# Two sums of a Strassen block written to PSUM, and the mixture's products issued in the order of the code

## The chip, the cores and the metric

The kernel runs on one core of a Trainium2 chip. Its engines work side by side: TensorE (PE in the profile, its weight loads PEld), VectorE (DVE), ScalarE (ACT), GpSimd (POOL) and SyncE (SP), which issues the DMA transfers. The metric is the device time of one execution in microseconds, lower is better; for the kernel before, the median of three runs is given.

## The reference

Banded attention with a few global columns gives x, 3072 tokens by 512; a mixture of eight experts follows, whose mixing weights are a matrix of token by expert, normalized alternately along its rows and columns, eight times.

```python
x = attention(q, k, v)                  # 4*768 tokens, 8 heads * 64
logits = x @ w_gate                     # 3072 x 8
P = np.exp(logits - logits.max())
for _ in range(8):
    P /= P.sum(1, keepdims=True) + 1e-09
    P /= P.sum(0, keepdims=True) + 1e-09
    P *= N / E
for e in range(8):
    h = np.maximum(x @ w1[e], 0.0)      # 3072 x 1024
    out += P[:, e:e + 1] * (h @ w2[e])  # 3072 x 512
```

## The kernel before

**Tiling.** The tokens are cut into eight units of 384 (`NU`, three tiles of 128 each), and two units make a block b. Every operand of a product is split into a high and a low half, so that each product is three matmuls: high by low, low by high, high by high (`products`, L617 to L619; `layer2`, L685 to L687). The attention comes first, with the first experts' work on units 0 to 6 woven between its steps. From about 380 us on only the mixture is left, in this order of the code in `pipeline`:

- **The last filler**, `filler(NU - 1, ...)`: for unit 7 and the first four column groups (f = 0 to 3) of expert 0, 48 matmuls into `h_ps` (384 columns each), four `relu_split`, then for each of three token tiles twelve matmuls into `y_ps` (512 columns, L698 to L700), each tile copied out by ScalarE (L810).
- **The gate** of unit 7: eight matmuls into `g_ps` (L710), a copy by ScalarE to `g_sb` (L713), three transposes (`gt_ps`, L717).
- **The loop over 120 steps.** A step takes one group g of weights (two column groups of an expert) and one block b. `layer1_strassen` computes the hidden values of the block's two units and the group's two column groups by Strassen's scheme: seven products m1 to m7, six matmuls of 384 columns each, 42 in all, into four PSUM banks in the order m3 to c, m2 to d, m1 to a, m6 to b, m5 to c, m4 to d, m7 to a. Between them ScalarE copies bank c (L658) and VectorE adds and subtracts (L660 to L671), and the four hidden blocks are split by `relu_split`: ScalarE's Relu gives the high half `hh` (L625), VectorE the low half `hl` (L626). `second` then does the second layer of the step before: six token tiles of six matmuls with 512 columns (36 in all) into `y_ps`, each added to its accumulator by VectorE (L933 for expert 0, L937 with the mixing weight for the others).
- **The normalization** `sinkhorn` is a generator of which `second` calls the next piece after the first, fourth and sixth tile. Each of its eight iterations is a chain on VectorE (L742 to L745, then L750 to L754) with one matmul between, `c_ps` (L748), which sums the columns over the partitions. When it is done, the accumulators of expert 0 are multiplied by its mixing weight on ScalarE, two blocks of six (L936).

**Pools.** The four banks a to d come from `mps` with four buffers, so the next step's banks are the same four; `yps` has three, `sps` (for g_sb's transposes and c_ps) one. `hpool` holds eight hh and eight hl.

**Weights.** Each group's weights are loaded by SyncE's queue into a single staging buffer, summed by GpSimd, cast to the high half by ScalarE (L537) and subtracted to the low half by GpSimd (L538), a step or two ahead.

**What sets the order.** Every instruction is recorded in the order of the code, and a scheduler then places the instructions of all engines by times that it estimates itself, unless one is held in the order of the code. `InOrder` does that: its `matmul` and `transpose` issue on TensorE and hold what they issue in program order. The attention uses it (`attention.pe`), and `moe.pe` is set to it while the attention runs; at L875 `moe.pe` becomes plain `nc.tensor`, so that the scheduler is free with the products of the mixture from there on. On each engine instructions start in the order in which they finally stand.

## Time and profile before

| what | value |
|---|---|
| median of 3 runs | 2286.73 us (2285.66 to 2288.38) |
| the profiled execution | 2288.16 us |
| its span in the trace | 2286.3 us |
| granted TensorE clock, mean | 0.989 of full speed |
| TensorE busy | 2236.0 us, 98% of the span |
| VectorE busy | 1560.3 us, 68% |
| GpSimd busy | 823.5 us, 36% |
| ScalarE busy | 696.2 us, 30% |
| chain that ended last, TensorE's share | 90% |
| first product of the loop's first step | starts at 398.98 us |

The span is the time from the first to the last instruction of one profiled execution. Busy shares are means over stages that differ; what an edit is worth is read in its own stage, from what TensorE waits for there. A row of the timeline gives start, duration, engine, line, operation and, in brackets, the idle time before it and who ended it. Durations of matmuls are modelled, and consecutive ones overlap; the distance from start to start is what a product costs. Matmuls carry the lines of the helper that issues them: L617 to L619 in `products`, L685 to L687 in `layer2`, L698 to L700 in `layer2_wide`.

### The profile page before, as it was taken

To read this page: it belongs to the slowest core of one execution; us is meant where nothing else is said; L and a number is where in the kernel's file an instruction comes from. 1 tells how busy PE (TensorE), PEld (TensorE's weight loads), DVE (VectorE), ACT (ScalarE), POOL (GpSimd) and SP (SyncE) were. 2 spreads that over 40 slices of the span, in tenths; PEclk is the share of its full clock that TensorE was granted. 3 is DMA by queue.
4 is the path that set the end of the run, shared out by engine and by line. 5 is a ranking of instruction groups with operands and counts; after the bars stand their busy time and mean duration, and the time that the engine had idled before them with its cause. 6 is when DMAs were issued, how large, how long until landed. Compare 5 with 4: busy or idle time off the path is not lost.

```text
span 2286.3 us, 31486 instructions
## 1 busy us (share of the span) xinstructions
PE 2236.0 (98%) x12147; PEld 1991.2 (87%) x12147; DVE 1560.3 (68%) x2746; ACT 696.2 (30%) x1528; POOL 823.5 (36%) x655
## 2 busy tenths in 40 slices
PE   7989989999999999999999999999999999999998
PEld 5777878898998998998998998998998999989987
DVE  6566666886766666766666667666766666666665
ACT  5655654332222222222222224222222222222221
POOL 4165283432333333333333234333333233333320
PEclk8999999999999999999999999999999999999999
DMA  6455433110111011111001361101110101110101
GB/s 163 116 163 145 125 85 95 32 43 28 37 38 38 28 30 36 38 37 37 28 29 38 129 239 39 36 28 38 37 38 28 37 28 38 37 37 28 35 22 57
DMA packets 177615, 133.75 MB, mean 59 GB/s; under 512 B 117040, under 2 KB 148784, under 8 KB 177456
## 3 DMA queue, kind: packets, MB, share of 16 engines
q1 hardware_dynamic: 177456, 131.65, 19.3%
q8 instruction: 97, 1.59, 0.3%
q14 instruction: 62, 0.51, 0.1%
HBM read 108.81 MB, written 22.81 MB: 58 GB/s over the span
## 4 chain that ended last, share of the span: by engine, by line
PE 90%; DVE 3%; issue 3%; POOL 2%; ACT 1%; DMA 0%; SPq 0%; DVEq 0%; POOLq 0%; ACTq 0%
PE y_ps L686 15%; PE y_ps L687 15%; PE y_ps L685 14%; PE bank_d L618 4%; PE bank_d L617 4%; PE bank_c L617 4%; PE bank_c L619 4%; PE bank_a L618 4%; PE bank_c L618 4%; PE bank_a L617 4%; PE bank_d L619 4%; PE bank_a L619 4%; PE bank_b L617 2%; PE bank_b L619 2%; PE bank_b L618 2%
## 5 line engine op out<-in xcount | busy, mean ns | idle before, releaser
L937 DVE SCALAR_TENSOR_TENSOR acc<-y_ps,pm,acc 128x512 f32<-128x512 f32 x672 | 500.2, 748 | 327.0 <-PE y_ps L687 324.5
L687 PE MATMUL y_ps<-w2h,hh 128*128 128x512 f32 x1440 | 567.5, 394 | 0.0
L686 PE MATMUL y_ps<-w2h,hl 128*128 128x512 f32 x1440 | 566.9, 394 | 0.0
L685 PE MATMUL y_ps<-w2l,hh 128*128 128x512 f32 x1440 | 561.9, 390 | 0.0
L538 POOL TENSOR_TENSOR w2l<-w2f,w2h 128x1024 fp32r<-128x1024 f32 x60 | 144.5, 2408 | 702.0 <-ACT w2h L537 702.0
L687 PEld LDWEIGHTS y_ps<-w2h,hh 128*128 128x128 f32 x1440 | 270.1, 188 | 53.7
L685 PEld LDWEIGHTS y_ps<-w2l,hh 128*128 128x128 f32 x1440 | 270.4, 188 | 43.5 <-DVE acc L937 0.2
L686 PEld LDWEIGHTS y_ps<-w2h,hl 128*128 128x128 f32 x1440 | 270.0, 188 | 43.4
L560 POOL TENSOR_TENSOR wsum<-w1f 128x256 f32<-128x256 f32 x300 | 225.5, 786 | 216.5 <-DMA w1f<-in_moe_w_dram 216.5
L538 POOL TENSOR_TENSOR wl<-wsum,wh 128x1280 fp32r<-128x1280 f32 x60 | 177.4, 2957 | 279.4 <-ACT wh L537 279.4
L625 ACT ACTIVATE hh<-h 128x384 fp32r<-128x384 f32 x120 | 63.1, 526 | 502.5 <-DVE h L665 501.1
L626 DVE SCALAR_TENSOR_TENSOR hl<-t,hh 128x384 fp32r<-128x384 f32 x120 | 165.1, 1376 | 10.2 <-ACT hh L625 10.1
L617 PE MATMUL bank_d<-xl,wh 128*128 128x384 f32 x480 | 160.9, 335 | 1.5 <-DVE t L671 1.5
L617 PE MATMUL bank_c<-xl,wh 128*128 128x384 f32 x480 | 161.9, 337 | 0.0
L619 PE MATMUL bank_c<-xh,wh 128*128 128x384 f32 x480 | 161.9, 337 | 0.0
L618 PE MATMUL bank_c<-xh,wl 128*128 128x384 f32 x480 | 161.2, 336 | 0.0
L618 PE MATMUL bank_d<-xh,wl 128*128 128x384 f32 x480 | 161.2, 336 | 0.0
L618 PE MATMUL bank_a<-sh,wl 128*128 128x384 f32 x480 | 161.1, 336 | 0.0
L617 PE MATMUL bank_a<-sl,wh 128*128 128x384 f32 x480 | 161.0, 335 | 0.0
L619 PE MATMUL bank_a<-sh,wh 128*128 128x384 f32 x480 | 160.8, 335 | 0.0
L619 PE MATMUL bank_d<-xh,wh 128*128 128x384 f32 x480 | 160.3, 334 | 0.0
L626 DVE SCALAR_TENSOR_TENSOR hl<-h,hh 128x384 fp32r<-128x384 f32 x120 | 110.1, 918 | 68.7 <-ACT hh L625 68.7
(195 smaller groups left out, 3960.1 us busy)
## 6 DMA issues: line engine op xcount, KB each, us to landing
w1f<-in_moe_w_dram SPq DMA_DIRECT2D x62, 512.0 KB, 3.4
w2f<-in_moe_w_dram SPq DMA_DIRECT2D x62, 512.0 KB, 3.7
out_dram<-acc SPq DMA_DIRECT2D x24, 256.0 KB, 2.2
ys<-y_sb SPq DMA_DIRECT2D x21, 256.0 KB, 2.1
acc<-ys SPq DMA_DIRECT2D x7, 768.0 KB, 4.3
acc<-in_q_dram SPq DMA_DIRECT2D x32, 96.0 KB, 2.5
acc<-in_k_dram SPq DMA_DIRECT2D x32, 96.0 KB, 2.7
acc<-in_v_dram SPq DMA_DIRECT2D x32, 96.0 KB, 2.2
```

Of the source, the lines that this page charges most:

```text
L538: self.nc.gpsimd.tensor_tensor(out=lo, in0=full, in1=hi, op=ALU.subtract)
L560: nc.gpsimd.tensor_tensor(out=s[:, n], in0=x, in1=y, op=op)
L617: self.pe.matmul(out, lhsT=hi(c), rhs=xlo(c), start=(first and c == 0), stop=False, skip_group_check=True)
L618: self.pe.matmul(out, lhsT=lo(c), rhs=xhi(c), start=False, stop=False, skip_group_check=True)
L619: self.pe.matmul(out, lhsT=hi(c), rhs=xhi(c), start=False, stop=(last and c == n - 1), skip_group_check=True)
L625: nc.scalar.activation(out=hh, in_=src, func=AF.Relu)
L626: self.latest = nc.vector.scalar_tensor_tensor(out=hl, in0=src, scalar=0.0, in1=hh, op0=ALU.max, op1=ALU.subtract)
L685: self.pe.matmul(y_ps, lhsT=hh[:, cols], rhs=lf, start=(f == 0), stop=False)
L686: self.pe.matmul(y_ps, lhsT=hl[:, cols], rhs=wf, start=False, stop=False)
L687: self.pe.matmul(y_ps, lhsT=hh[:, cols], rhs=wf, start=False, stop=(f == n - 1))
L937: nc.vector.scalar_tensor_tensor(out=a, in0=y_ps, scalar=moe.pm[:, tt, e:e + 1], in1=a, op0=ALU.mult, op1=ALU.add)
```

## The change

Two edits. In `layer1_strassen` the last sum of h22 is written into bank b instead of the SBUF tile, and the last sum of t3 into bank a; `relu_split` reads these two hidden blocks from the banks, as it did the other two before. And the line that gave `moe.pe` back to `nc.tensor` is gone, so every product and transpose of the mixture goes through `InOrder` to the end of the program.

```diff
@@ layer1_strassen
         product("m6", "b", True, True)
-        tt(out=h22, in0=b, in1=h22, op=ALU.add)
+        tt(out=b, in0=b, in1=h22, op=ALU.add)
         product("m5", "c", False, True)
         product("m4", "d", False, True)
         tt(out=t3, in0=d, in1=t3, op=ALU.add)
         tt(out=t3, in0=t3, in1=c, op=ALU.subtract)
         product("m7", "a", False, True)
-        tt(out=t3, in0=a, in1=t3, op=ALU.add)
-        r22 = self.relu_split(h22, hpool)
+        tt(out=a, in0=a, in1=t3, op=ALU.add)
+        r22 = self.relu_split(b, hpool)
         r12 = self.relu_split(c, hpool)
         r21 = self.relu_split(d, hpool)
-        r11 = self.relu_split(t3, hpool)
+        r11 = self.relu_split(a, hpool)
@@ pipeline
         attention.flush()
         for _ in todo:
             pass
-        moe.pe = nc.tensor
         att.close()
```

In the changed program the lines behind L875 have numbers lower by one (L933 is L932), and all matmuls stand under L83, `InOrder.matmul`.

**In the loop, on TensorE.** `bank_a` to `bank_d` are the first layer's banks, `y_ps` the second layer's. In the program before, the two layers are mixed:

```order
L687 MATMUL y_ps<-w2h,hh 128x512
L617 MATMUL bank_c<-xl,wh 128x384
L618 MATMUL bank_c<-xh,wl 128x384
...
L618 MATMUL bank_a<-sh_4089,wl 128x384
L685 MATMUL y_ps<-w2l,hh 128x512
...
L687 MATMUL y_ps<-w2h,hh 128x512
L619 MATMUL bank_a<-sh_4089,wh 128x384
L685 MATMUL y_ps<-w2l,hh 128x512
```

After it, the 36 of a second layer stand together and the 42 of a first layer follow; its second-layer piece ends thus:

```order
L83 MATMUL y_ps<-w2l,hh 128x512
L83 MATMUL y_ps<-w2h,hl 128x512
L83 MATMUL y_ps<-w2h,hh 128x512
L83 MATMUL bank_c<-xl,wh 128x384
L83 MATMUL bank_c<-xh,wl 128x384
```

The switch from one width of product to the other came about ten times a step before and now comes twice.

**In the last filler, on TensorE.** The first tile's bank is `y_ps_5200`, the second's `y_ps_5214`; the pairs hh_5145 and hl_5146, hh_5162 and hl_5163 belong to f = 0 and f = 1, hh_5179 and hl_5180 to f = 2. Before, the second tile's products stand between those of the first, and so ahead of those that need f = 1:

```order
L698 MATMUL y_ps_5200<-w2l_852,hh_5145 128x512
L699 MATMUL y_ps_5200<-w2h_851,hl_5146 128x512
L700 MATMUL y_ps_5200<-w2h_851,hh_5145 128x512
L698 MATMUL y_ps_5200<-w2l_852,hh_5162 128x512
L698 MATMUL y_ps_5214<-w2l_852,hh_5145 128x512
L699 MATMUL y_ps_5214<-w2h_851,hl_5146 128x512
L699 MATMUL y_ps_5200<-w2h_851,hl_5163 128x512
```

Now the first tile goes through all four f before the second begins:

```order
L83 MATMUL y_ps_5200<-w2l_852,hh_5162 128x512
L83 MATMUL y_ps_5200<-w2h_851,hl_5163 128x512
L83 MATMUL y_ps_5200<-w2h_851,hh_5162 128x512
L83 MATMUL y_ps_5200<-w2l_864,hh_5179 128x512
L83 MATMUL y_ps_5200<-w2h_863,hl_5180 128x512
```

The gate's eight matmuls moved as well: ahead of the filler's 48 into h_ps before, behind the filler's 36 into y_ps now. On ScalarE the copy of g_sb (L713) stood ahead of all of the last filler's copies and now stands behind the three copies of L810, three casts of `wh` and one of `w2h` (L537).

**In the normalization, on VectorE.** `csum`, `rsum` and `pm` belong to it, `hl` are low halves of a first layer, `acc` accumulations of a second. The same stretch of the chain, from the reciprocal of one iteration's column sums to the scaled rows, before:

```order
L752 RECIPROCAL csum_5617<-csum_5617 128x8
L933 TENSOR_TENSOR acc_63<-y_ps_5520,acc_63 128x512
L753 TENSOR_SCALAR csum_5617<-csum_5617 128x8
L660 TENSOR_TENSOR t3_5547<-t3_5547,bank_d_5538 128x384
L754 TENSOR_TENSOR pm_120<-pm_120,csum_5617 128x192
L663 TENSOR_TENSOR h22_5562<-bank_a_5539,t3_5547 128x384
L742 TENSOR_REDUCE rsum_5623<-pm_120 128x24
```

and now:

```order
L752 RECIPROCAL csum_5617<-csum_5617 128x8
L626 SCALAR_TENSOR_TENSOR hl_5605<-bank_a_5539,hh_5604 128x384
L932 TENSOR_TENSOR acc_63<-y_ps_5637,acc_63 128x512
L753 TENSOR_SCALAR csum_5617<-csum_5617 128x8
L754 TENSOR_TENSOR pm_120<-pm_120,csum_5617 128x192
L932 TENSOR_TENSOR acc_63<-y_ps_5645,acc_63 128x512
L742 TENSOR_REDUCE rsum_5623<-pm_120 128x24
```

The instructions of the chain keep their order; what stands between them changed, and on TensorE the c_ps of an iteration stands at its place in the code, 18 and 12 products of 512 columns apart within a second layer, with nothing of the next first layer ahead of it. On ScalarE eleven of the twelve multiplications of L936 and a cast of `w2h` now stand ahead of a copy of bank c (L658), where two such copies stood ahead of all twelve before.

## The prediction

> **What bounds the kernel now.** I read the page first (busy time, then the chain that ended last), then the waits, then the windows by stage, then the timeline where the windows raised a question. From the page, the span, the busy times and the chain by engine:

> ```profile
> span 2286.3 us, 31486 instructions
> PE 2236.0 (98%) x12147; PEld 1991.2 (87%) x12147; DVE 1560.3 (68%) x2746; ACT 696.2 (30%) x1528; POOL 823.5 (36%) x655
> PE 90%; DVE 3%; issue 3%; POOL 2%; ACT 1%; DMA 0%; SPq 0%; DVEq 0%; POOLq 0%; ACTq 0%
> ```

> TensorE is busy 98% of the span and carries 90% of the chain; VectorE, second, has 68%. So edits on VectorE pay only where TensorE waits for VectorE, and time must come from how densely matmuls follow one another. The list of waits and two windows of the core, with the bounds, their length, TensorE (busy, matmuls), weight loads, VectorE, ScalarE, GpSimd, the granted clock, the DMA share and GB/s (ten steps of the loop, then a stretch of the last products):

> ```profile
> PE bank_d L617 <- DVE t L671: 1.5, 2, 1.2
> PE y_ps L699 <- DVE hl L626: 0.8, 1, 0.8
> 1236.17:1392.58 156.41, 156.41 (x781) 140.83 (x780) 106.29 (x161) 41.00 (x75) 50.30 (x45) 1.00 0.39 142
> 2267.00:2277.00 10.00, 10.00 (x46) 8.27 (x45) 6.14 (x9) 0.32 (x1) 0.00 (x0) 1.00 0.09 34
> ```

> From the first step at 399 us on, TensorE hardly waits: the largest wait for a bank is 1.5 us in the whole run. A step (42 products of 384 columns, 36 of 512) takes 156.41/10 = 15.64 us at full clock. Inside it the spacing depends on neighbours. From the timeline of TensorE (start, duration as modelled, product), a run of 512-column products, the switch, and twelve products of 384; then two rows from the end of the program:

> ```profile
> 1014.27 0.39 PE L687 MATMUL y_ps<-w2h,hh 128*128 128x512 f32 x1
> 1016.35 0.39 PE L687 MATMUL y_ps<-w2h,hh 128*128 128x512 f32 x1
> 1017.26 0.33 PE L617 MATMUL bank_c<-xl,wh 128*128 128x384 f32 x1
> 1018.33 0.33 PE L617 MATMUL bank_d<-xl,wh 128*128 128x384 f32 x1
> 1019.37 0.33 PE L617 MATMUL bank_a<-sl,wh 128*128 128x384 f32 x1
> 2268.22 0.39 PE L685 MATMUL y_ps<-w2l,hh 128*128 128x512 f32 x1
> 2269.35 0.39 PE L687 MATMUL y_ps<-w2h,hh 128*128 128x512 f32 x1
> ```

> The first two rows lie nine starts apart: 2.08/9 = 231 ns. The next four starts take 0.91, 227 each; deep in the long run at the end, five take 1.13, 226. After the switch six 384s take 1.07, 178 each; the next six 1.04, 173. A product thus costs 4 to 5 ns more at the first six to nine places of a run of its width.

> **The change part by part.** *Sums into banks.* VectorE's low halves (group rows: count, then busy and mean ns, then idle before):

> ```profile
> L626 DVE SCALAR_TENSOR_TENSOR hl<-t,hh 128x384 fp32r<-128x384 f32 x120 | 165.1, 1376 | 10.2 <-ACT hh L625 10.1
> L626 DVE SCALAR_TENSOR_TENSOR hl<-h,hh 128x384 fp32r<-128x384 f32 x120 | 110.1, 918 | 68.7 <-ACT hh L625 68.7
> L626 DVE SCALAR_TENSOR_TENSOR hl<-bank_c,hh 128x384 fp32r<-128x384 f32 x120 | 66.3, 552 | 31.0 <-ACT hh L625 31.0
> ```

> With the input in SBUF one takes 1376 or 918 ns, from a bank 552. 120 × (1376 − 552) + 120 × (918 − 552) = 143 us go from VectorE; no wait of TensorE hangs on them but the 1.5 us, so I cost them at nothing, apart from that wait. Banks a and b now come free only after their low half. The next step needs the first bank 36 × 0.2267 = 8.2 us after the last first-layer product; four high halves, four low halves (4 × 0.55) and two or three accumulations are done in some 5. Cost 0; the third rival prices its failure.

> *Order, the loop.* In traced order every run has 42 or 36 products. 42 × 173.3 + 36 × 226.7 ns = 15.44 us; the 384s after the switch add about 5 ns six times, the 512s 4 ns nine times, 0.07 in all: 15.51 against 15.64, so −0.13 a step. Of the 120 steps the first few are disturbed: 115 × 0.13 = **−15.0**; −11 if a run's start costs half as much again, −23 if nothing. [...]

> *Order, the start.* Last filler and gate, around TensorE, VectorE's four low halves, ScalarE's copies:

> ```profile
> 379.53 0.34 PE L710 MATMUL g_ps<-xl,ghl 128*128 128x384 f32 x1
> 380.92 0.34 PE L617 MATMUL h_ps<-xl,w1h 128*128 128x384 f32 x1
> 389.27 0.39 PE L698 MATMUL y_ps<-w2l,hh 128*128 128x512 f32 x1
> 391.04 0.54 DVE L626 SCALAR_TENSOR_TENSOR hl<-h_ps,hh 128x384 fp32r<-128x384 f32 x1
> 393.77 0.55 DVE L626 SCALAR_TENSOR_TENSOR hl<-h_ps,hh 128x384 fp32r<-128x384 f32 x1
> 395.19 0.55 DVE L626 SCALAR_TENSOR_TENSOR hl<-h_ps,hh 128x384 fp32r<-128x384 f32 x1
> 398.80 0.59 ACT L810 COPY acc<-y_ps 128x512 f32<-128x512 f32 x1 [0.28 <-PE y_ps L700]
> 399.40 1.26 ACT L537 CAST wh<-wsum 128x1280 fp32r<-128x1280 f32 x1
> 402.13 0.47 ACT L658 COPY t<-bank_c 128x384 f32<-128x384 f32 x1
> 384.17 0.46 ACT L713 COPY g_sb<-g_ps 16x384 f32<-16x384 f32 x1
> 398.98 0.45 PE L617 MATMUL bank_c<-xl,wh 128*128 128x384 f32 x1
> ```

> The gate's eight products (379.53 to 380.92) stood ahead of the 48 h_ps; now they follow the 36 y_ps, so h_ps ends 1.39 earlier, at 387.9. That wins nothing: the first tile now takes f = 0, 1, 2, 3 in turn with nothing in between, and the low halves of f = 1, 2, 3 are ready at 391.6, 394.3, 395.7, set by VectorE's order, which is unmoved here. So this tile ends at 395.74 + 3 × 0.23 = 396.4, two more tiles take 24 × 0.228 = 5.5 (401.9), the gate 1.4 (403.3). ScalarE's copy of g_sb now stands behind the third L810 (to 402.4) and the casts (402.13 − 399.40 = 2.73, to 405.1); with its 0.46 it ends at 405.6, and the three transposes let bank_c start at 406.0 instead of 398.98: **+7.0**. Without the casts in its way it is +5; one more cast in between, +8.5.

> *Order, the normalization.* c_ps needs pm from VectorE, and TensorE now stands at it with every later product queued behind. The chain of an iteration in the trace, where it ran nearly undisturbed, an accumulation's group, and the worst instance of L745 with GpSimd's instruction beside it:

> ```profile
> 437.38 0.49 PE L748 MATMUL c_ps<-pm,ones 128*128 128x192 f32 x2
> 438.75 0.34 DVE L750 TENSOR_REDUCE csum<-c_ps 128x8 f32<-128x192 f32 x1
> 441.82 0.36 DVE L745 TENSOR_TENSOR pm<-pm,rsum 128x192 f32<-128x192 f32 x1
> L933 DVE TENSOR_TENSOR acc<-y_ps,acc 128x512 f32<-128x512 f32 x48 | 32.6, 682 | 13.1 <-PE y_ps L687 13.0
> L745 DVE TENSOR_TENSOR pm<-pm,rsum 128x192 f32<-128x192 f32 x8 | 6.0, 750 | 0.1
> 450.98 3.05 DVE L745 TENSOR_TENSOR pm<-pm,rsum 128x192 f32<-128x192 f32 x1
> 450.86 2.95 POOL L538 TENSOR_TENSOR wl<-wsum,wh 128x1280 fp32r<-128x1280 f32 x1 [4.18 <-ACT wh L537]
> ```

> L750 to the end of L745 is 442.18 − 438.75 = 3.43 with one accumulation in it (0.6), so 2.8 alone. Between two c_ps of one second layer stand 18 or 12 products, 4.1 or 2.75 us, and the c_ps itself, 0.33. The first interval of a step holds in VectorE's order, beside the chain, some three low halves (0.5 each) and three or four accumulations (0.6): 2.8 + 1.5 + 2.1 + 0.2 for the hand-overs = 6.6, against 4.4: 2.2 of waiting. The second: 2.8 + 2.0 + 0.2 = 5.0 against 3.1: 1.9. The eight c_ps lie three, three and two to a step, the first of each covered by 42 first-layer products: five waits, 2.2 + 1.9 + 2.2 + 1.9 + 2.2 = 10.4. L745 averages 750 ns where it is alone 360, and stretched to 3.05 us beside GpSimd's 2.95: I add 0.7 a wait, together **+14**. Bounds: 8.5 (no stretching, one accumulation fewer in each) and 17. [...]

> *Order, ScalarE's scaling.* Twelve accumulators are scaled once pm is final:

> ```profile
> 493.25 0.49 PE L748 MATMUL c_ps<-pm,ones 128*128 128x192 f32 x2
> 493.97 0.45 PE L617 MATMUL bank_d<-xl,wh 128*128 128x384 f32 x1 [0.24 <-DVE t L671]
> 496.33 0.34 DVE L754 TENSOR_TENSOR pm<-pm,csum 128x192 f32<-128x192 f32 x1
> 496.71 7.48 ACT L936 ACTIVATE acc<-acc,pm 128x512 f32<-128x512 f32 x12 [2.56 <-DVE pm L754]
> 409.49 0.44 PE L617 MATMUL bank_d<-xl,wh 128*128 128x384 f32 x1 [1.23 <-DVE t L671]
> ```

> Twelve take 7.48. In the changed order eleven of them (6.9) and a weight cast (1.3) stand ahead of the copy of bank c (L658, 0.47) which the product m5 waits for. From the last c_ps to the end of L754 it takes 496.67 − 493.25 = 3.4, then 8.2 on ScalarE and 0.5 for the copy: 12.1. TensorE has 18 products of 512 and 24 of 384 until m5, 8.3: it waits 3.8, less the 0.4 lost here before (bank_d starts 0.72 after c_ps, which itself takes 0.33): **+3.4** (2 to 5). Bank_d's wait in the second step, 1.23, falls to about 0.4, since bank a is read from the bank: −0.9; the first accumulations meet VectorE's operand sums of the last block: +0.5 (0 to 3). Together −0.4.

> **The sum**: −15.0 + 7.0 + 14.0 + 3.4 − 0.4 = **+9.0**. The profiled execution took 2288.16 (span 2286.3 and 1.9 around it), 1.43 above the median of the runs; it goes to 2297.2, the median 2286.73 to **2295.7**.

> **The rivals.** *One: VectorE gets through the chain between two c_ps.* If accumulations and low halves do not fall between its instructions, 2.8 + 0.2 us fit under 4.4 and nearly under 3.1; the five waits shrink to about 1.5 in all, pm is final 1.8 us sooner, ScalarE's term falls to 1.5: −15 + 7 + 1.5 + 1.5 − 0.4 = −5.4, **2281.3**, faster. It decides at 4.4 us from c_ps to pm. For it: 3.43 in the row above. Against: the order's rows, with a low half and two accumulations among four instructions of the chain. 0.07.

> *Two: spacing is by width alone*, and the 4 ns in the rows come from something that stays, such as whose turn it is among the weight loads. Then the loop gains 0 and the start still pays 24: **2310.7**. Against: it shows in both widths, at the position in the run. 0.06.

> *Three: banks come free too late in every step.* The four low halves are done after 8.2 us instead of 5, since accumulations stand between; each half microsecond beyond costs 115 × 0.5 = 58, with the nine 67: **2353.2**. For it: TensorE no longer has other products to put in. Against: VectorE's 106.29 busy in ten steps, 68%, falls by 1.2 a step. 0.03. That the order does not become strict is excluded by the rows of the order.

> **How the numbers follow.** My forecast has 0.84. Its ends: the loop −11 to −23, start 5 to 8.5, normalization 8.5 to 17, scaling 2 to 5, rest −1 to +2; all ends at once give −8.5 and +21.5. They are independent, so the likely band is about ±6; with the rivals' 0.16 beyond, the range is 2287 to 2305. About 0.2%, 4.6 us, is what a measurement of this kernel can tell from no change. Below +4.6 lies 0.13 of the forecast's 0.84, below −4.6 some 0.01: faster 0.08 (rival one and this), same 0.13, slower 0.79 (0.70 and rivals two and three).

> **What would show it.** Right: steps of 15.51 us in the middle of the run; bank_c of the first step at about 406; five waits at L748 of 2 to 3.5 us and one of 3 to 4 at m5 (L617 into bank_c) near the last c_ps; no bank waits later. Wrong: steps still at 15.64 (rival two), waits at L748 below 1 us (rival one), waits for L626 at L617 in every step (rival three), or a first step that starts on time.

## The result, and the profile after

The changed kernel takes 2300.84 us in the median of five runs (2298.59 to 2307.01), the kernel before, with the runs beside it, 2288.32 (2285.66 to 2290.14). The ratio is 1.0061, with a 95% interval of 1.0048 to 1.0073: 11 to 17 us slower. The forecast was 2295.7, nine more than before, in a range of 2287 to 2305.

The page of the changed kernel, span, busy times and chain by engine:

```profile
span 2299.0 us, 31428 instructions
PE 2232.3 (97%) x12147; PEld 1994.2 (87%) x12147; DVE 1446.5 (63%) x2746; ACT 676.7 (29%) x1528; POOL 794.8 (35%) x655
PE 89%; DVE 4%; issue 3%; POOL 2%; ACT 2%; DMA 1%; SPq 0%; ACTq 0%; DVEq 0%; POOLq 0%
```

VectorE lost 114 us of work, and the kernel became slower. Windows of the changed kernel (columns as in the prediction): ten steps in the middle of the run, the stretch from the start of the last filler to the first step, the first ten steps, and two short windows inside these.

```profile
1199.33:1354.39 155.06, 155.06 (x781) 140.62 (x780) 96.85 (x160) 35.35 (x69) 48.99 (x44) 1.00 0.30 106
380.88:409.29 28.41, 22.20 (x97) 18.15 (x95) 16.73 (x12) 10.03 (x17) 22.84 (x14) 0.88 0.23 74
409.29:579.06 169.77, 154.99 (x765) 138.12 (x764) 118.28 (x236) 44.50 (x84) 55.39 (x49) 0.98 0.11 34
396.30:400.60 4.30, 4.30 (x11) 3.10 (x10) 2.84 (x4) 1.32 (x2) 4.30 (x5) 0.50 0.00 0
451.00:455.20 4.20, 4.20 (x12) 3.27 (x11) 3.20 (x8) 0.00 (x0) 2.96 (x5) 0.50 0.00 0
```

Ten steps take 155.06 instead of 156.41: 15.51 each, as forecast. The spacing inside a step, behind a switch from 512 to 384 columns (timeline):

```profile
1028.75 0.33 PE L83 MATMUL bank_c<-xl,wh 128*128 128x384 f32 x1
...
1029.82 0.33 PE L83 MATMUL bank_d<-xl,wh 128*128 128x384 f32 x1
...
1030.86 0.33 PE L83 MATMUL bank_a<-sl,wh 128*128 128x384 f32 x1
```

Six starts take 1.07, the next six 1.04: 178 and 173 ns, the very figures of before. The places of a run cost what they did; there are only fewer first places. The mean spacing of the middle of the run says the same: from the seventh place of a run on it is 173.3 ns, from the tenth on 226.7, in the changed kernel as before. The other two long windows, of the kernel before; its first begins with the gate's eight products, which stood ahead of the filler there and stand inside the stretch now:

```profile
379.53:398.98 19.45, 18.63 (x97) 16.44 (x95) 16.81 (x12) 6.92 (x13) 18.56 (x12) 1.00 0.33 109
398.98:548.15 149.17, 147.69 (x747) 133.68 (x746) 120.02 (x233) 48.85 (x89) 60.00 (x49) 1.00 0.12 36
```

So the start went from 19.45 to 28.41, +9.0, and the first ten steps from 149.2 to 169.8, +20.6. From there to the last product it is 1732.08 before and 1713.66 after, −18.4 (last product at 2280.23 and 2292.72). In the last two figures 4.2 us is the same work at another place: before, the second layer lags behind the first and is made up at the end (27.65 us from the last step's first product to the last product, 23.44 now). The real loss in the first ten steps is 16.4, the gain behind them 14.2.

All in all this is +11.15 from the start of that stretch to the last product. The remaining 1.35 of the profiles lies in the attention ahead of it, which is the same code: over the thirteen profiles of this study that stretch started anywhere between 371.6 and 384.8 us. From there on the two profiles of the changed kernel agree to 0.1 us (1911.85 and 1911.96). The table of runs below therefore gives both: the median, which holds the attention's scatter, and "from the filler", the time in the one profile of each run from the first product of the last filler or its gate, whichever comes first, to the last product.

The waits of TensorE in the changed kernel that are not the attention's (us in total, times, longest):

```profile
PE c_ps L83 <- DVE pm L745: 11.1, 5, 3.2
PE y_ps L83 <- DVE hl L626: 3.8, 3, 2.1
PE bank_c L83 <- ACT t L658: 3.3, 1, 3.3
PE gt_ps L86 <- ACT g_sb L713: 2.4, 1, 2.4
PE bank_d L83 <- DVE hl L626: 0.3, 1, 0.3
```

Five waits at c_ps, three for the low halves, one at m5, one at the gate, nothing later: the places that the prediction named. The timeline of the start, TensorE and ScalarE:

```profile
389.22 0.40 PE L83 MATMUL y_ps<-w2l,hh 128*128 128x512 f32 x1
...
392.94 0.50 PE L83 MATMUL y_ps<-w2h,hl 128*128 128x512 f32 x1 [2.08 <-DVE hl L626]
...
395.65 0.79 PE L83 MATMUL y_ps<-w2h,hl 128*128 128x512 f32 x1 [1.44 <-DVE hl L626]
...
399.35 0.63 PE L83 MATMUL y_ps<-w2l,hh 128*128 128x512 f32 x1
399.78 0.63 PE L83 MATMUL y_ps<-w2h,hl 128*128 128x512 f32 x1
...
405.08 0.34 PE L83 MATMUL g_ps<-xl,ghl 128*128 128x384 f32 x1
408.48 0.46 ACT L713 COPY g_sb<-g_ps 16x384 f32<-16x384 f32 x1
409.00 0.35 PE L86 MATMUL gt_ps<-ident,g_sb 16*128 16x16 f32 x3 [2.36 <-ACT g_sb L713]
```

The waits for the low halves and for g_sb are there. New is what stands between them: from 396.2 to 401.1 products of 512 columns start 427 ns apart (399.35 to 399.78), not 227; the window 396.30:400.60 above shows the granted clock at 0.50. Eleven products lost 2.2 us that way. The first wait of the normalization shows the same:

```profile
449.63 0.36 DVE L745 TENSOR_TENSOR pm<-pm,rsum 128x192 f32<-128x192 f32 x1
450.14 0.98 PE L83 MATMUL c_ps<-pm,ones 128*128 128x192 f32 x2 [3.21 <-DVE pm L745]
450.66 0.88 PE L83 MATMUL y_ps<-w2l,hh 128*128 128x512 f32 x1
...
451.77 0.63 PE L83 MATMUL y_ps<-w2h,hh 128*128 128x512 f32 x1
452.19 0.63 PE L83 MATMUL y_ps<-w2l,hh 128*128 128x512 f32 x1
```

TensorE waits 3.21 us for pm, and ten of the next products run at half clock, 2.0 us lost. The scaling on ScalarE and the product behind it:

```profile
496.77 6.85 ACT L935 ACTIVATE acc<-acc,pm 128x512 f32<-128x512 f32 x11 [8.20 <-DVE pm L754]
503.53 1.03 ACT L537 CAST w2h<-w2f 128x1024 fp32r<-128x1024 f32 x1
504.46 0.72 ACT L935 ACTIVATE acc<-acc,pm 128x512 f32<-128x512 f32 x1
505.08 0.46 ACT L658 COPY t<-bank_c 128x384 f32<-128x384 f32 x1
505.59 0.44 PE L83 MATMUL bank_c<-xl,wh 128*128 128x384 f32 x1 [3.34 <-ACT t L658]
```

All twelve multiplications (one more than the eleven that the order was said to have there) and the cast come ahead of the copy, and m5 waits 3.34 us for it.

### The profile page after: what moved, and what is told of

The parts are those of the page before. It is cut to its first block, busy times and chain, and to the rows that moved or that the text cites. A ratio compares the mean times of both kernels' runs of the same rounds, so it can differ in the third digit from the quotient of the medians.

```text
span 2299.0 us, 31428 instructions
## 1 busy us (share of the span) xinstructions
PE 2232.3 (97%) x12147; PEld 1994.2 (87%) x12147; DVE 1446.5 (63%) x2746; ACT 676.7 (29%) x1528; POOL 794.8 (35%) x655
## 4 chain that ended last, share of the span: by engine, by line
PE 89%; DVE 4%; issue 3%; POOL 2%; ACT 2%; DMA 1%; SPq 0%; ACTq 0%; DVEq 0%; POOLq 0%
PE y_ps L83 44%; PE bank_c L83 11%; PE bank_d L83 11%; PE bank_a L83 11%; PE bank_b L83 5%; PE h_ps L83 2%; PE s_ps L83 1%; PE o_ps L83 1%; PE t_ps L86 1%; PE tp L86 1%; ACT p_sb L291 1%; DVE xl L385 1%; POOL xsum L610 0%; DVE inv L297 0%; PE r_ps L86 0%
## 5 line engine op out<-in xcount | busy, mean ns | idle before, releaser
L936 DVE SCALAR_TENSOR_TENSOR acc<-y_ps,pm,acc 128x512 f32<-128x512 f32 x672 | 502.7, 748 | 258.6 <-PE y_ps L83 258.6
L83 PE MATMUL y_ps<-w2h,hl 128*128 128x512 f32 x1536 | 602.6, 392 | 3.8 <-DVE hl L626 3.8
L83 PE MATMUL y_ps<-w2l,hh 128*128 128x512 f32 x1536 | 604.6, 394 | 0.1
L83 PE MATMUL y_ps<-w2h,hh 128*128 128x512 f32 x1536 | 602.3, 392 | 0.0
L538 POOL TENSOR_TENSOR w2l<-w2f,w2h 128x1024 fp32r<-128x1024 f32 x60 | 144.3, 2406 | 667.2 <-ACT w2h L537 667.2
L83 PEld LDWEIGHTS y_ps<-w2h,hl 128*128 128x128 f32 x1536 | 289.6, 189 | 61.3 <-DVE hl L626 5.4
L83 PEld LDWEIGHTS y_ps<-w2h,hh 128*128 128x128 f32 x1536 | 289.5, 188 | 60.8
L83 PEld LDWEIGHTS y_ps<-w2l,hh 128*128 128x128 f32 x1536 | 289.6, 189 | 56.8 <-ACT hh L625 0.5
L538 POOL TENSOR_TENSOR wl<-wsum,wh 128x1280 fp32r<-128x1280 f32 x60 | 177.8, 2963 | 354.5 <-ACT wh L537 354.5
L537 ACT CAST w2h<-w2f 128x1024 fp32r<-128x1024 f32 x60 | 63.2, 1053 | 380.3 <-PE y_ps L83 366.6
L660 DVE TENSOR_TENSOR t<-t,bank_d 128x384 f32<-128x384 f32 x120 | 66.5, 554 | 171.6 <-PE bank_d L83 164.8
L625 ACT ACTIVATE hh<-bank_b 128x384 fp32r<-128x384 f32 x120 | 59.1, 492 | 390.8 <-DVE bank_b L665 390.8
L658 ACT COPY t<-bank_c 128x384 f32<-128x384 f32 x120 | 57.8, 482 | 378.2 <-PE bank_c L83 377.6
L83 PE MATMUL bank_c<-xl,wh 128*128 128x384 f32 x480 | 162.2, 338 | 3.3 <-ACT t L658 3.3
L83 PE MATMUL bank_c<-xh,wh 128*128 128x384 f32 x480 | 161.9, 337 | 0.0
L83 PE MATMUL bank_c<-xh,wl 128*128 128x384 f32 x480 | 161.2, 336 | 0.0
L83 PE MATMUL bank_d<-xl,wh 128*128 128x384 f32 x480 | 160.4, 334 | 0.3 <-DVE hl L626 0.3
L83 PE MATMUL bank_d<-xh,wl 128*128 128x384 f32 x480 | 160.3, 334 | 0.0
L83 PE MATMUL bank_d<-xh,wh 128*128 128x384 f32 x480 | 160.3, 334 | 0.0
L83 PE MATMUL bank_a<-sl,wh 128*128 128x384 f32 x480 | 160.3, 334 | 0.0
L83 PE MATMUL bank_a<-sh,wl 128*128 128x384 f32 x480 | 160.3, 334 | 0.0
```

The lines of the kernel that those rows point to most:

```text
L83: return self.tc.keep_in_program_order(self.engine.matmul(*args, **kw))
L537: self.nc.scalar.copy(out=hi, in_=full)
L538: self.nc.gpsimd.tensor_tensor(out=lo, in0=full, in1=hi, op=ALU.subtract)
L625: nc.scalar.activation(out=hh, in_=src, func=AF.Relu)
L658: nc.scalar.copy(out=t3, in_=c)
L660: tt(out=t3, in0=t3, in1=d, op=ALU.subtract)
```

## The experiments

The theory is the prediction's, with what the profile added: the time moved with the order alone; the loop gains 0.13 us a step because a run of one width costs extra at its first places (178 against 173 ns at 384 columns, 231 against 227 at 512); the loss lies in the start, the normalization and the scaling, where TensorE stands in strict order behind VectorE and ScalarE; and TensorE's clock falls to half when it has idled (granted 0.50 behind the waits of 1.44 and 3.21 us shown above). Rivals: the loop gained from VectorE's lighter load; the half clock is chance; the loss is spread over the run.

Each ratio is to runs of the kernel before on the same chip.

| run | median, us | ratio to before (95%) | from the filler, us |
|---|---|---|---|
| before | 2288.32 | | 1900.70 |
| the change | 2300.84 | 1.0061 (1.0048 to 1.0073) | 1911.85 |
| e1 sums only | 2287.91 | 1.0001 (0.9992 to 1.0010) | 1900.68 |
| e2 order only | 2300.93 | 1.0059 (1.0045 to 1.0072) | 1911.70 |
| e3 order from step 8 | 2277.10 | 0.9959 (0.9946 to 0.9973) | 1890.81 |
| e4 start moved | 2293.93 | 1.0027 (1.0015 to 1.0039) | 1906.65 |
| e5 waits filled, in part | 2302.68 | 1.0063 (1.0048 to 1.0078) | 1914.99 |
| e6 c_ps spread | 2287.32 | 0.9993 (0.9984 to 1.0002) | 1900.08 |
| e7 e4 and e6 | 2279.74 | 0.9954 (0.9940 to 0.9969) | 1893.06 |
| e8 half runs | 2307.72 | 1.0084 (1.0068 to 1.0099) | 1920.90 |
| e9 waits filled, all | 2300.04 | 1.0046 (1.0032 to 1.0060) | 1911.70 |
| e10 order from step 11 | 2272.74 | 0.9935 (0.9921 to 0.9949) | 1886.08 |
| e11 the change again | 2300.34 | 1.0052 (1.0038 to 1.0066) | 1911.96 |

### One half of the change at a time

e1 keeps the sums in the banks and gives the order back to the scheduler:

```diff
             pass
+        moe.pe = nc.tensor
         att.close()
```

> The two sums in PSUM banks, with the order of the products left free as before. Theory (the time moved with the order alone; the sums cost and bring nothing): steps of 15.62 to 15.70 us, first product of the loop at 398 to 401 us, total within 5 us of the kernel before (2283 to 2293). Rival (the step got shorter because VectorE has 143 us less to do): steps of 15.51 us here too, total 2270 to 2276.

e2 is the kernel before without its line `moe.pe = nc.tensor`.

> The traced order, with the two sums in SBUF as before. Theory: steps of 15.51 us, the same waits at the start and at the normalization, total 2296 to 2306, about as the changed kernel. Rival (strict order needs the cheaper low halves, or else the banks and hidden values come late in each step): waits of TensorE at the first layer's banks in every step, steps above 15.6 us, total above 2312.

Ten steps of each, e1 and then e2:

```profile
1173.18:1329.58 156.40, 156.40 (x781) 140.77 (x780) 95.70 (x161) 36.36 (x69) 49.54 (x47) 1.00 0.27 95
```

```profile
1196.92:1351.99 155.07, 155.07 (x782) 140.61 (x780) 98.47 (x160) 35.94 (x69) 50.53 (x44) 1.00 0.29 106
```

In e1 VectorE is busy 95.7 us in ten steps instead of 106, and the steps are 15.64 us long as before; from the filler the time is the same to 0.02 us. In e2 the steps are 15.51 and the total is the changed kernel's. The sums are worth nothing in either order, and the whole effect is the order's. The rival of each falls.

### The order later

e3 and e10 leave the order free through the start and the normalization:

```diff
+        moe.pe = nc.tensor
         att.close()
...
         for n, (g, b) in enumerate(steps):
+            if n == 7:                  # e10: 10
+                moe.pe = attention.pe
             hs = moe.layer1_strassen(...)
```

> The sums in banks; the order is left free in the last filler, the gate and the first seven steps, and is as in the code from the eighth step on. Theory (all of the loss lies in the start, the normalization and the scaling; all of the gain in the runs of one width): first product of the loop at 398 to 401 us, steps of 15.51 us after the change of order, total 2286.7 - 14.6 = 2270 to 2277. Rival (the loss is spread over the run): 2285 or more.

e3 came out at 2277.1, 0.1 us above its range, and from the filler it takes 9.9 less than before, where 14.6 was expected. Its list of waits has one that is in neither kernel:

```profile
PE y_ps L685 <- DVE acc L937: 4.7, 1, 4.7
```

At the change of order 54 products of the second layer are still to be done, and their accumulations stand behind the scaling. That this wait belongs to the place, not to the strict order as such, e10 tests:

> As the third run, with the order of the code from the eleventh step on instead of the eighth, when the second layer has caught up. Theory (the third run lost 4.7 us to one wait at the change of order, since 54 products of the second layer stood there behind the scaling): that wait is at most 1.2, steps of 15.51 us from the eleventh on, 109 x 0.13 = 14.2 less than before, total 2272 to 2276. Rival (the wait moves along with the change of order): a wait of 4 us or more there, total 2277 to 2280.

e10 has no such wait, takes 14.6 less than before from the filler (forecast 14.2) and is the fastest kernel of the study: 2272.74, a ratio of 0.9935 (0.9921 to 0.9949). Loss and gain of the change can thus be separated by place.

### The start and the normalization

e4 moves the gate's products ahead of the last filler and takes the filler's three tiles in turn for each f, by hand, as the scheduler had done:

```diff
+        last_gate = moe.gate(NU - 1, xs[NU - 1], sps, "s")
+        next(last_gate)
         for _ in filler(NU - 1, ...): pass
-        for _ in moe.gate(NU - 1, xs[NU - 1], sps, "s"): pass
+        for _ in last_gate: pass
...
+            if dst is not None:
+                ys = [ps2.tile([P, DM], F32, name="y_ps", tag=tag2) for t in range(UT)]
+                tiles = [moe.layer2_wide(t, ws, hs, ys[t]) for t in range(UT)]
+                for _ in range(NF0):
+                    for tile_of in tiles:
+                        next(tile_of, None)
+                for t in range(UT):
+                    nc.scalar.copy(out=dst[:, t], in_=ys[t])
+                return
```

> The changed kernel, with the gate's products traced ahead of the last filler and the filler's second layer traced with the three tiles in turn for each f. Theory: the waits for the low halves and for g_sb go and with them the slow clock of the changed kernel at 396 to 401 us; the loop's first product at 398 to 400.5 us instead of 409.3, the rest as it was: about 2290.5 (2287 to 2295). Rival (another wait takes their place, such as bank c or the operands' sums on VectorE): first product above 404 us, total above 2296.

The start takes 19.2 us instead of 28.4, but only 5.2 of these 9.2 remain at the end. The first ten steps take 173.8 instead of 169.8, mainly for two reasons: the second layer's first tiles wait 1.0 us for accumulations, which now meet VectorE's operand sums, and the half clock costs 4.5 us there instead of 2.0 (17 slow products behind the wait of 3.4 us at m5, which had none before). The total, 2293.9, is inside the range and at its upper end.

e6 calls the normalization's pieces at other places:

```diff
         tt(out=b, in0=b, in1=h22, op=ALU.add)
+        if hook is not None:            # sinkhorn, from the third step on
+            next(hook, None)
...
-                    if t == 0 or i * t == 2:
+                    if (t == 0 or i * t == 2) if s == 0 else (i == t):
                         next(sinkhorn, None)
```

> The changed kernel, with the normalization's pieces called at the middle of the first layer and after the first and fifth tile of the second layer, so that 4.5 to 5.5 us of other products stand between two c_ps. Theory (a wait is the chain on VectorE less the cover on TensorE): waits at c_ps fall from 11.1 us to 2 to 5 in all, no half clock there, the scaling's wait from 3.3 to below 2, total 2287 to 2292. Rival (the chain stretches with the time given, since other work fills VectorE in between): waits of 2 us or more at five c_ps, total above 2296.

e6's waits at c_ps and at m5:

```profile
PE c_ps L83 <- DVE pm L747: 4.6, 6, 1.1
PE bank_c L83 <- ACT t L658: 0.7, 1, 0.7
```

They fell from 11.1 and 3.3, no product behind them runs at half clock, and 11.8 us are won from the filler. The chain does not stretch with the time it is given. e7 joins both edits:

> The fourth and the sixth run's edits together. Theory: the gains add, 2276 to 2282, below the kernel before. Rival (an earlier start shifts VectorE's and ScalarE's other work into the chains): 2285 or more.

Behind 380 us it runs at half clock nowhere (granted clock 1.00 in its start and its first ten steps), and the gains add (5.2 + 11.8 = 17.0; measured 18.8, from the filler). At 2279.7 it is below the kernel before with the strict order everywhere: the loss of the change came from where the code places three things (the gate with the filler's tiles, the normalization's pieces, and the scaling behind them), not from the strict order as such.

### The length of runs

e8 makes the steps' order itself shorter-grained: from the tenth step on 24, 18, 18, 18.

```diff
+        between()                       # first half of the step before's second layer
         product("m5", "c", False, True)
...
+                if i == 1 and n > 8:    # in second: the other half comes behind m7
+                    yield
```

> The changed kernel, with the order of the code itself changed from the tenth step on: 24 first-layer products, 18 of the second layer, 18, 18. Theory (a run's first places cost 26 ns in all for 384 columns and 40 for 512): steps of 15.51 + 0.066 = 15.57 us, total 2300.8 + 7 = 2308 if no bank comes late. Rival (spacing by width alone, and the gain came from elsewhere): steps of 15.51 us, total as the changed kernel. If a bank comes late, it shows as waits at the first layer's banks, and the spacing is read from the undisturbed runs.

Ten steps of e8:

```profile
1201.82:1357.55 155.73, 155.73 (x781) 140.85 (x780) 95.95 (x161) 35.37 (x69) 48.95 (x45) 1.00 0.30 107
```

The same 78 products, no wait, full clock, 15.573 us a step: 0.066 more for one more pair of runs, just what the first places of a run cost (26 + 40 ns), and the places themselves cost in e8's runs of 18 and 24 what they cost in runs of 36 and 42: 178 ns at the first six of 384 columns, 231 at the first nine of 512. Spacing by width alone (the prediction's second rival) would have left 15.51.

### The clock

e5 and e9 put useless products, into a bank of the normalization that nothing reads, where TensorE would wait:

```diff
+        def busy(count):
+            ...
+            d_ps = sps.tile([P, UNIT], F32, name="d_ps", tag="s")
+            for c in range(count):
+                moe.pe.matmul(d_ps, lhsT=moe.ghl[:, 0], rhs=xs[NU - 1][0][:, 0], ...)
...
+            busy((0, 18, 9, 0, 18, 8, 0, 9)[k])   # e9: (0, 19, 12, 0, 19, 20, 0, 13)
             c_ps = ps.tile([P, TT, E], F32, name="c_ps", tag=tag)
```

> The changed kernel with useless products put into TensorE's waits: 11, 8 and 2 ahead of the first filler tile's f = 1, 2, 3, and 18, 9, 18, 8, 9 ahead of the five c_ps that waited, all 384 columns wide into the normalization's own bank. The output is unchanged. Theory (the clock fell to half because TensorE stood idle): no products at 427 ns from 380 us on, total 4 to 6 us below the changed kernel, 2294 to 2298. Rival (the clock fell by chance or by something else): 427 ns products appear as before, total as the changed kernel, 2298 to 2306.

The half-clock stretches at 396 and 451 us went, but three others came, behind waits that e5 had left or not filled enough (2.4 us at the gate, 2.5 at a c_ps, 3.4 at m5): they cost 4.5 us, against 4.2 in the first profile. So e5 does not decide it; the total did not fall, and from the filler it rose by 3.1. e9 fills all:

> As the fifth run, with useless products in every wait of the start, the normalization and the scaling: 15 ahead of the gate's transposes, 19, 12, 19, 20 and 13 ahead of the five c_ps, 20 ahead of m5 in the sixth step (the gate's two tiles lie in the first layer's pool for that). The output is unchanged. Theory (the clock falls to half only after TensorE has idled 1.6 us or more): no products at half clock from 380 us on, total 3 to 5 us below the changed kernel run beside it, 2296 to 2298; the useless products themselves cost nothing as long as they end before the wait does. Rival (half clock comes at these places whether TensorE idles or not): half-clock stretches of 10 or more products, total as the changed kernel.

> The changed kernel once more, on the chip of the ninth and tenth run: 2297 to 2304. Both theories of the ninth run expect half-clock stretches here, 2 to 6 us of them in all; their places may differ from the first profile's.

From the filler's first product to the first step, then the first ten steps: e9, then e11, the changed kernel beside it.

```profile
384.76:411.44 26.68, 25.80 (x132) 22.66 (x131) 16.78 (x12) 10.03 (x17) 23.09 (x14) 1.00 0.24 79
411.44:582.80 171.36, 170.27 (x869) 154.33 (x867) 119.81 (x236) 44.48 (x84) 56.05 (x49) 1.00 0.11 33
```

```profile
382.12:409.47 27.35, 21.14 (x97) 17.35 (x95) 16.71 (x12) 10.04 (x17) 22.85 (x14) 0.94 0.24 77
409.47:580.42 170.95, 158.41 (x765) 141.28 (x764) 119.56 (x236) 44.51 (x84) 55.34 (x49) 0.96 0.11 33
```

With no wait left above 0.43 us, e9's granted clock is 1.00 in both windows and no product is slow; with the same waits unfilled, 31 products in five stretches are, which costs 5.7 us. So the half clock comes of TensorE's idle time; which of the first profile's waits brought it is read from the clock records in the last section. The 1.6 us in e9's theory is an estimate that e9, without such a wait, does not test. The price of the half clock is not what the theory said. The start gained (28.4 and 27.3 to 26.7), the normalization did not, and the totals are alike (2300.04 and 2300.34). What took the gain is on VectorE and GpSimd in e9 (L747 there is L745):

```profile
480.30 2.00 DVE L747 TENSOR_TENSOR pm<-pm,rsum 128x192 f32<-128x192 f32 x1
```

```profile
479.69 2.39 POOL L538 TENSOR_TENSOR w2l<-w2f,w2h 128x1024 fp32r<-128x1024 f32 x1 [0.70 <-ACT w2h L537]
```

This instruction takes 0.35 us elsewhere; here it meets GpSimd's subtraction and takes 1.65 more, in a chain on which TensorE waits. In the first profile of the changed kernel VectorE's instruction started 0.2 us ahead of GpSimd's:

```profile
478.80 0.35 DVE L745 TENSOR_TENSOR pm<-pm,rsum 128x192 f32<-128x192 f32 x1
```

```profile
479.00 2.38 POOL L538 TENSOR_TENSOR w2l<-w2f,w2h 128x1024 fp32r<-128x1024 f32 x1 [0.35 <-ACT w2h L537]
```

The useless products reach 0.2 to 0.5 us past three of the five pm, 0.9 in all. With the 1.65 that makes 2.5 us, while the half clock that e9 removed from these steps is 2.0 us of the first profile and 4.7 of e11. Against the first profile 1.1 of the 1.6 us by which e9's ten steps are longer stays unexplained. Against e11 the sum closes, since 2.4 us of its half clock was cover: its c_ps behind the slow products at 475 us waits 0.31 us, where the first profile has 1.45, and its m5, behind those at 496, 2.10 instead of 3.34. In the normalization the chain on VectorE sets the time, and the products between two c_ps, at half clock or full, are in part its cover.

## Why the prediction held, and where its terms were off

The forecast was right in direction, range and places; the sum, +9.0, was below the measured +12.5 (interval 11 to 17).

*Sums into banks*, 0: right. The two low halves now read from banks (group rows of the changed kernel):

```profile
L626 DVE SCALAR_TENSOR_TENSOR hl<-bank_b,hh 128x384 fp32r<-128x384 f32 x120 | 66.8, 557 | 73.5 <-ACT hh L625 73.5
L626 DVE SCALAR_TENSOR_TENSOR hl<-bank_a,hh 128x384 fp32r<-128x384 f32 x120 | 65.4, 545 | 0.2 <-ACT hh L625 0.2
```

165.1 + 110.1 − 66.8 − 65.4 = 143.0, the 143 of the forecast (VectorE's busy time, in which overlapping instructions count once, fell by 114). They brought nothing: e1 equals before.

*Order, the loop*, −0.13 a step: right to a hundredth, 15.507 against 15.637, −14.2 behind the tenth step. e8 shows that the first places of a run carry it.

*Order, the start*, +7.0: measured +9.0. The low halves, the casts and the gate went as written. What failed is the step "two more tiles take 24 × 0.228 = 5.5": the prediction priced waits as waits, and behind two of them eleven products ran at half clock, 2.2 us.

*Order, the normalization*, +14: the five waits were 11.1, not 14, since the stretch of L745 that I added to each (0.7) did not occur in this profile (353 ns on average, 750 before). The half clock behind the first wait, 2.0, came in its place: two errors offset one another, which is luck. e9, where the clock does not fall and one L745 is stretched, shows that they do not move independently. The waits are not distributed as forecast either. Behind 18 products of 512 columns they are 3.2, 3.2 and 1.8 us where 2.2 was forecast for each, behind 12 they are 1.5 where 1.9 was; only two of the five lie in the 2 to 3.5 us that the prediction named as its sign. The upper bound of 17 no run shows: the waits at c_ps add up to 11.4 at most, in e8.

*Order, ScalarE's scaling*, +3.4: 3.3 at m5, but by luck. The last c_ps stands behind the fourth tile, so that 12 products of 512 columns, not 18, come between it and the next first layer: 12 × 0.2267 + 24 × 0.1733 = 6.9 us of cover instead of 8.3. And from that c_ps (494.73) to the end of L754 (496.74) it takes 2.0 us instead of 3.4. The two errors of 1.4 cancel. *The small terms*: bank_d's wait fell to 0.3 as forecast (the prediction's "largest wait for a bank is 1.5 us in the whole run" is the total of two, the longer 1.2, and holds only for the loop); the second layer's first tiles lost nothing here, but 1.0 in e4, where the start is earlier. Together, normalization, scaling and small terms were forecast at 17.0, less 0.13 a step in these steps; measured 16.4 with that in it.

The half clock, which the prediction put at nothing, could have been foreseen. Behind 380 us no wait of the kernel before is longer than 1.2 us and none is followed by slow products (granted clock 1.00 up to the last product). But its attention shows it: behind a wait of 1.97 us, products of 384 columns start 320 ns apart, at a granted clock of 0.50.

```profile
228.21 0.90 PE L86 MATMUL t_ps<-ident,p_sb 128*128 128x128 f32 x6 [1.97 <-DVE kl L240]
...
229.69 0.52 PE L83 MATMUL h_ps<-xl,w1h 128*128 128x384 f32 x1
230.01 0.52 PE L83 MATMUL h_ps<-xh,w1l 128*128 128x384 f32 x1
```

The rest of the difference to the median lies in the attention's scatter.

Open stays what in TensorE makes the first six to nine products of a run slower: the runs show that it follows the position and costs 26 ns for 384 columns and 40 for 512, not why.

## What to carry to other kernels

Strict program order and a scheduler's order have different prices at different places: look for the stretch where the busiest engine depends on a chain elsewhere, leave that free (or place its pieces by hand, as e7 does), and order strictly where nothing waits; here that turned 11 us lost into 15 won, from the filler. A change of matmul width inside a saturated stream cost 26 ns (to 384 columns) and 40 ns (to 512) here, so long runs are worth having in a loop that runs a hundred times. And a wait of a saturated TensorE is to be priced with the products behind it: here 21 of them ran at half clock, 4.2 us in the changed kernel's first profile. That price is not due where they are themselves the cover of the next wait.

## What the runs showed of the hardware

From 380 us to the last product, the first profile of the changed kernel has two stretches at half clock (granted 0.50, products of 512 columns 427 instead of 227 ns apart). Ahead of the first lie two idle times of TensorE, of 2.08 and 1.44 us with three products between, ahead of the second one of 3.21 us; in e3 the wait of 4.7 us is followed by products 427 ns apart. Not every such idle time has one: of the changed kernel's two waits of 3.21 us at c_ps the first is followed by slow products in the first profile, and the second is not; in e11 both are (granted clock 0.96 in the first ten steps, where the first profile has 0.98).

```profile
445.77:449.18 3.41, 1.16 (x6) 0.62 (x4) 3.34 (x10) 0.00 (x0) 1.14 (x2) 1.00 0.31 103
449.18:452.59 3.41, 2.45 (x6) 2.15 (x7) 2.04 (x8) 0.00 (x0) 2.22 (x4) 0.50 0.14 51
469.67:473.08 3.41, 1.65 (x8) 1.03 (x6) 3.38 (x9) 0.00 (x0) 1.63 (x3) 1.00 0.14 36
473.08:476.49 3.41, 1.96 (x9) 1.73 (x10) 2.46 (x9) 0.00 (x0) 1.47 (x3) 1.00 0.35 120
```

The first wait leaves 2.25 us of one interval idle, and the next interval has half clock; a bound of the grid cuts the second wait into 1.76 and 1.45, and nothing follows. From 380 us to the last product this trace has two intervals at full clock with more idle time than 1.79 us, this one of 2.25 and one of 2.18 from 391.16, and these two are followed by half clock, no other one is. In the trace of the kernel before no interval there has more than 1.23, and no half clock comes. This was read from the traces afterwards and holds for the saturated part of these two executions alone. Among the attention's smaller products the same count does not separate them: an interval with 1.47 us idle, from 49.83 in the first profile, is followed by half clock, one with 1.50, from 61.94 in the kernel before, is not.
